# An outer product moved from VectorE into one more matmul of each of the first 32 items, with a new order of steps

## The chip, the core and the metric

The kernel runs on one core of a Trainium2 chip. The metric is device time in microseconds (us): the median of three executions, 1103.94 us, with a lowest of 1103.72 and a highest of 1105.09. The engines are called PE (TensorE matmuls), PEld (TensorE weight loads), DVE (VectorE), ACT (ScalarE), POOL (GpSimd) and SP (SyncE, which here only issues transfers).

## What is computed

The reference is a real part of a two-dimensional Fourier transform, followed by two feed-forward layers:

```
X   = fft(fft(x, axis=1), axis=2).real            # x: 2 x 3008 x 256
x1  = X.reshape(6016, 256)
h   = x1 @ w_in                                   # 256 x 2048
y   = (h * clip(h + 3, 0, 6) / 6) @ w_out         # 2048 x 256
xn  = y / sqrt(mean(y*y) + 1e-6) * rms_g
out = (silu(xn @ w_gate) * (xn @ w_val)) @ w_out2 # 256 x 1536, 1536 x 256
```

The transform along the 256 columns is folded into `w_in` (function `wmm`, L302): the 256 columns become 128 cosine-like ones and 128 sine-like ones, and one column is left over, number 128. Its contribution to the even half E of a hidden unit f is a rank-one term: (row 128 of the transformed weight at f) times (column 128 of the folded input at each token). That term is what the change is about.

## The kernel before, in words

**Precision.** Every product is made of three matmuls of split numbers (`PASSES`, L35): high part by high part, high by low, low by high. A high part is a copy rounded to the matmul type (ACT writes it), a low part is the difference (`sub`, L271, on POOL, or on DVE where a step in the list carries an apostrophe, L748).

**Stages.** First the input is folded and split (`fold`, L350, `sums`, L329), the transform's matrices are converted (`conv_mat`, L234), and small matmuls make the sequence transform (`pmm`, `xmm`, L443 to L447), evacuated by `evac` (L449) and `evac_x` (L464). Meanwhile the four 512-column chunks of `w_in` and of `w_out` are decoded from 64-bit floats on ACT and DVE (`decode`, L254) and those of `w_in` are transformed by `wmm`. Then 96 items of the first layer run (`item1`, L526): six blocks of 502 tokens by 16 groups of 128 hidden units. The order of the items (L523) is block 0 with groups 0 to 7, block 1 with all 16, block 0 with groups 8 to 15, then blocks 2 to 5. So items 0 to 31 are blocks 0 and 1. Then 144 items of the second layer follow (`item2`, L682), with `rms` (L631) between.

**One item of the first layer.** Three matmuls into a PSUM bank E and three into a bank O (L536), then on DVE T = x128 * w128 + E (L540, `scalar_tensor_tensor`, the rank-one term), E = T + O and O = T - O (L542, L543); ACT makes two Relu passes into R (L548), DVE two clip-and-multiply passes (L551), ACT the rounded copy HI (L554), POOL two subtractions into LO (L559), and 12 matmuls go from HI and LO into four accumulating banks (L570). There are two E/O pairs, two T, two R, two HI and two LO buffers, used in turn.

**Column 128.** `fold_x128`, `split_x128` and `xmm` make the transformed column in both batches at once: partitions 0 to 63 hold the first batch, 64 to 127 the second. `evac_x` writes it into `xb[0]` (tile PQX0) and issues three transfers on SP for each parity of frequencies (L476 to L478): two copy the second batch's half to both halves of `xb[1]` (tile X1), and the third overwrites the lower half of `xb[0]`, once the first two have read it. The weights of column 128 are row 0 of the bank `o` in `wmm`: ACT copies it to a T buffer (L313), SP writes it to a DRAM row (L315) and reads it back as the per-partition scalars `wx` (L322).

**The order of the work.** Every task is a Python generator, and the list `STEPS` (L78 to L166) says by hand which task takes its next step. All engines' queues get their instructions in that order. A planner wrote the list. The number alone is a step of a first-layer item, `+n` one of the second layer.

Of the kernel before, what the change touches and what calls it, by code (L numbers as in the profile page):

```python
# [76 lines left out]
}  # L77
STEPS = """  # L78
    one dm x01 x01 raw00 xq x00 x00 lwi0 raw01 raw02 x02 x02 raw11 raw10 fold1 fold1 fold1 fold1 fold1 mat00 mat00 fx
    fold1 mat00 sx0 fold0 fold1 fold0 sx0 fold1' sx0 fold0 X00 fold1 fold0 fold1 fold0 dwi0 fold1' fold0 dwi0 fold0 mat01  # L80
    fold0' mat01 dwi0 PQ100 mat01 mat02 fold0 dwi0 mat02 X01 fold0 fold2 lwi1 mat02 fold0' dwi0 PQ101 fold2 fold2 X02
    dwi0' mat11 mat11 PQ000 fold2 lwo0 evx0 fold2 wt0 mat11 mat10 evx0 wt0 mat10 fold2 evx0 mat10 PQ001 fold2 wt0 fold2'
    wt0 wt0 fold2 PQ102 wt0 wt0 fold2 wt0 PQ002 ev10 fold2' dwo0 ev10 raw12 PQ010 dwo0 ev00 wt0 ev00 PQ011 dwo0 pq00 PQ110
    mat12 dwo0 PQ111 mat12 pq00' dwo0 PQ012 mat12 dwo0' ev01 PQ112 ev01 dwi1 lwo1 0 ev11 dwi1 ev11 dwi1 1 0 sx1 dwi1 sx1
    sx1 0 dwi1 X10 1 0 dwi1 1 X11 lwi2 0 1 X12 lwi3 lwo3 wt1 0 1 pq01 0 2 evx1 1 0 evx1 wt1 dwo1 2 1 2 0 wt1 1 wt1 wt1
    dwo1 2 evx1 pq01 dwi3 2 1 dwi3 2 wt1 wt1 2 lwo2 3 g wt1 wt1 2 3 4 dwi3 2 3 dwi3 3 4 3 4 5 3 dwo1 3 4 5 4 3 5 6 4 dwo1
    4 5 3 6 dwo1 5 4 6 7 5 dwo1 6 7 7 5 4 dwi2 6 5 dwi2 7 8 dwi2 6 5 7 6 dwi2 6 9 8 7 8 7 6 9 8 7 9 8 9 7 8 9 dwi2 8 10 9
    8 7 11 10 9 10 9 8 11 10 dwi2 11 10 11 9 dwo2 11 10 dwo2 10 wt2 11 dwo2 12 10 g wt2 12 11 12 10 wt2 dwi3 11 wt2 wt2
    dwi3' 12 wt2 11 wt2 wt2 12 wt2 12 dwo2 wt3 dwo3 12 13 12 dwo2 wt3 13 13 12 wt3 lm00 wt3 dwo2' wt3 13 wt3 wt3 13 wt3
    x10 wt3 14 13 dwo3 13 15 14 14 13 15 14 13 15 14 15 dwo3 14 16 15 14 16 17 15 14 16 15 14 17 16 15 17 16 17 15 16 17  # L90
    16 dwo3 18 16 17 19 dwo3 18 18 17 16 19 17 18 19 dwo3 18 19 17 18 19 18 lf0 20 19 18 21 20 lf0 19 18 21 20 19 21 20 19
    lf0 21 20 x11 lf0 22 20 lf0 20 21 22 20 23 21 22 21 20 pq02 23 21 23 22 pq02 23 22 21 23 22 22 lf1 24 23 22 25 24 lf1
    23 22 25 24 23 25 24 23 25 24 25 24 26 23 lf1 24 27 26 x12 25 26 24 27 25 24 26 27 25 26 27 lf1 28 26 27 25 26 28 28
    26 29 lf1 27 lf2 28 27 26 29 28 27 29 30 28 lf2 29 28 27 30 29 28 30 31 29 30 29 28 31 31 29 30 31 29 30 31 30 lf2 32
    30 31 33 32 32 31 30 33 32 31 33 32 33 31 32 33 32 lf2 34 33 32 31 35 ls00 33 34 33 32 35 lf2 34 lm01 35 33 34 ls00 35
    34 35 34 36 34 35 gr00 36 34 36 35 36 34 35 ls10 36 gr00 lm02 ls10' gr00 37 36 36 38 37 37 36 35 38 37 38 37 38 36 37
    38 37 39 38 37 40 39 38 39 37 38 40 39 40 39 40 38 39 40 39 41 40 39 42 41 40 41 39 40 42 41 42 41 42 40 41 42 41 43
    42 41 44 43 42 43 41 42 44 43 44 43 44 42 43 44 43 45 44 43 gr10 45 44 45 44 45 43 lm10 gr10 45 ls01 gr10 lm11 46 pq10
    45 pq10' 47 45 46 44 47 45 46 ls01 47 46 45 47 46 47 46 48 46 47 gr01 48 47 48 46 47 48 46 lm12 gr01 48 ls11 gr01 49
    48 48 47 49 49 48 ls11' 49 50 lw00 47 49 50 gr11 49 50 49 50 49 48 50 cw00 gr11 cw00 gr11 51 50 cw00 cw00 pq11 50 52  # L100
    51 lw10 cw00 lw01 51 50 49 52 51 cw00 52 51 52 50 51 52 51 53 52 51 54 53 52 53 51 52 54 53 54 53 54 52 53 54 rms2 53
    55 54 rms2 53 56 55 55 pq11 53 56 55 56 54 cw01 55 54 cw01 57 55 56 55 54 57 56 55 57 58 56 cw01 57 cw01 56 55 58 lw11
    cw01 57 56 cw01' 59 57 58 cw10 57 56 59 58 cw10 57 59 58 57 59 cw10 58 59 58 60 cw10 59 58 61 lw20 cw10 60 60 cw10 58
    61 60 59 cw10 61 cw11 59 60 59 61 cw11 60 cw11 61 60 62 cw11 61 60 lw21 cw11 63 62 62 61 60 63 cw11 62 63 61 cw20 cw11
    62 61 63 cw20 62 cw20 63 62 64 cw20 63 62 cw20 65 64 64 63 62 65 cw20 64 65 63 cw21 cw20 64 63 65 cw21 64 cw21 65 64
    66 63 cw21 64 67 66 65 66 64 cw21 65 67 66 67 65 rms0 66 cw21 65 67 66 cw21 67 66 rms0 68 67 66 69 68 68 67 66 69 67
    68 69 68 69 67 68 69 68 70 69 68 71 70 69 70 68 69 71 70 71 70 71 69 70 71 rms0 70 rms0 72 71 70 73 72 72 71 70 73 71
    72 73 72 73 71 72 73 72 rms0 73 74 72 rms0 75 rms0 73 74 rms0 72 74 73 75 74 rms0 75 73 rms0 75 74 rms0 75 74 76 pq12
    rms0 74 77 76 75 76 74 77 75 74 76 77 75 76 pq12 77 78 76 77 75 rms1 76 78 78 76 79 rms1 77 rms0 78 77 76 79 rms0 79
    77 78 79 77 rms0 78 79 78 rms0 80 79 78 rms0 81 79 80 78 81 79 80 81 80 79 rms0 81 80 lw30 rms0 81 80 82 rms0 79 80 83  # L110
    82 82 cw30 80 81 83 80 82 cw30 81 83 81 82 cw30 81 83 cw30 82 lw40 83 82 84 83 82 85 84 83 84 82 83 85 84 85 84 85 83
    84 85 84 86 85 84 87 86 85 86 84 cw30 85 87 86 cw30' 87 85 86 87 86 87 86 88 87 86 rms1 89 88 88 tw1 86 87 89 88 87 89
# [736 lines left out]
```

## Time and profile before

| what | value |
|---|---|
| median of 3 executions | 1103.94 us (1103.72 to 1105.09) |
| the profiled execution | 1106.04 us |
| its span, first to last instruction | 1104.1 us |
| its mean granted TensorE clock | 0.992 of full speed |
| PE busy in the span | 1056.1 us, 4572 matmuls |
| DVE, ACT, POOL busy | 774.9, 537.5, 501.0 us |

Read the profile in this order: busy time by engine over the whole span, then busy time by stretch, then, for the stretch in which items 0 to 31 run, the idle time ahead of each group of matmuls and what ended it, then the chain of waits. The profiled execution is 1.94 us outside its span and 2.10 us above the median.

### The profile page before, as it was taken

How to read it: one execution, taken by the hardware profiler on the slowest of the kernel's cores; microseconds unless marked ns; L12 is line 12 of the kernel's file. 1: busy time of each engine (PE TensorE's matmuls, PEld its weight loads, DVE VectorE, ACT ScalarE, POOL GpSimd, SP SyncE). 2: the span in 40 equal slices, each digit the busy share in tenths (PEclk: the TensorE clock that was granted, in tenths of full speed). 3: DMA queues.
4: the chain of work that ended last, by engine and by line, in shares of the span. 5: the costliest groups of instructions: out<-in, count | busy, mean ns of one | idle time of the engine just before them, and what ended most of it. 6: DMA issues, size and time to landing. Idle time of an engine off the chain costs nothing.

```text
span 1104.1 us, 12691 instructions
## 1 busy us (share of the span) xinstructions
PE 1056.1 (96%) x4572; PEld 865.2 (78%) x4572; DVE 774.9 (70%) x1173; ACT 537.5 (49%) x814; POOL 501.0 (45%) x384
## 2 busy tenths in 40 slices
PE   3789898999999999999999999999999999999998
PEld 3668777888887877777878888888888888888886
DVE  7799999987889989887687574454554456364532
ACT  5556555555656666654445343333333344343332
POOL 0057477767676766654534333332323333332332
PEclk9899999999999999999999999999999999999999
DMA  8450401042502100111310000000000000000000
GB/s 294 136 173 1 80 12 65 1 83 47 129 7 96 39 0 20 39 39 44 109 58 20 19 1 20 2 17 19 1 19 1 19 8 12 19 1 20 1 19 20
DMA packets 19175, 47.21 MB, mean 43 GB/s; under 512 B 3942, under 2 KB 7014, under 8 KB 18478
## 3 DMA queue, kind: packets, MB, share of 16 engines
q1 hardware_dynamic: 16088, 36.92, 10.2%
q0 software_dynamic: 3024, 9.48, 3.8%
q8 instruction: 36, 0.59, 0.2%
q14 instruction: 27, 0.22, 0.1%
HBM read 33.53 MB, written 8.27 MB: 38 GB/s over the span
## 4 chain that ended last, share of the span: by engine, by line
PE 67%; DVE 19%; POOL 5%; issue 3%; ACT 3%; DMA 2%; SPq 0%; DVEq 0%; ACTq 0%; POOLq 0%
PE acc L715 16%; PE E L693 16%; PE O L693 16%; PE acc L570 12%; POOL LO L272 4%; PE E L536 3%; PE O L536 3%; DVE R L551 3%; DVE T L540 2%; DVE O L543 2%; DVE E L542 2%; ACT HI L554 1%; PE E L439 1%; PE O L439 1%; DMA J<-in_x 1%
## 5 line engine op out<-in xcount | busy, mean ns | idle before, releaser
L272 POOL TENSOR_TENSOR LO<-R,HI 128x502 fp32r<-128x502 f32 x192 | 260.9, 1387 | 143.9 <-ACT HI L554 143.9
L570 PE MATMUL acc<-HI,B 128*128 128x502 f32 x768 | 248.4, 392 | 0.0
L699 DVE TENSOR_TENSOR R<-T,E 128x502 f32<-128x502 f32 x144 | 97.2, 675 | 201.1 <-ACT T L696 187.7
L272 POOL TENSOR_TENSOR HI<-R,HI 128x502 fp32r<-128x502 f32 x87 | 116.6, 1340 | 231.7 <-ACT HI L705 231.5
L570 PEld LDWEIGHTS acc<-HI,B 128*128 128x128 f32 x768 | 145.4, 189 | 30.6 <-POOL B L272 0.3
L570 PE MATMUL acc<-LO,B 128*128 128x502 f32 x384 | 151.2, 394 | 2.1 <-POOL LO L272 2.0
L693 PE MATMUL E<-J,B 128*128 128x502 f32 x576 | 147.9, 392 | 1.0 <-DVE R L699 1.0
L693 PE MATMUL O<-J,A 128*128 128x502 f32 x576 | 147.5, 391 | 1.1 <-DVE R L701 1.1
L272 POOL TENSOR_TENSOR LO<-R,LO 128x502 fp32r<-128x502 f32 x57 | 76.5, 1342 | 155.7 <-ACT LO L705 155.5
L554 ACT CAST HI<-R 128x1004 fp32r<-128x1004 f32 x96 | 99.0, 1033 | 66.2 <-PE acc L570 33.1
L696 ACT ACTIVATE T<-E 128x502 f32<-128x502 f32 x144 | 84.5, 588 | 94.4 <-PE E L693 94.2
L693 PEld LDWEIGHTS E<-J,B 128*128 128x128 f32 x576 | 108.6, 189 | 25.2 <-DVE R L699 2.6
L693 PEld LDWEIGHTS O<-J,A 128*128 128x128 f32 x576 | 108.9, 189 | 24.3 <-DVE R L701 1.5
L548 ACT ACTIVATE R<-E,c_three 128x502 f32<-128x502 f32 x96 | 65.4, 681 | 98.8 <-DVE E L542 65.4
L705 ACT CAST HI<-R 128x502 fp32r<-128x502 f32 x87 | 53.4, 613 | 112.3 <-DVE R L701 91.3
L701 DVE TENSOR_TENSOR R<-R,O 128x502 f32<-128x502 f32 x144 | 97.4, 676 | 11.7
L536 PE MATMUL E<-J,A 128*128 128x502 f32 x288 | 84.8, 403 | 14.6 <-DVE R L551 10.1
L715 PE MATMUL acc<-HI,B 128*128 128x502 f32 x354 | 89.7, 390 | 0.0
L570 PEld LDWEIGHTS acc<-LO,B 128*128 128x128 f32 x384 | 72.9, 190 | 19.9 <-POOL LO L272 4.9
L536 PE MATMUL O<-J,A 128*128 128x502 f32 x288 | 83.4, 399 | 0.8 <-DVE A L320 0.8
L536 PEld LDWEIGHTS E<-J,A 128*128 128x128 f32 x288 | 53.4, 192 | 33.3 <-DVE R L551 16.7
L715 PEld LDWEIGHTS acc<-HI,B 128*128 128x128 f32 x354 | 66.9, 189 | 14.0
(234 smaller groups left out, 1605.1 us busy)
## 6 DMA issues: line engine op xcount, KB each, us to landing
out_dram<-H SPq DMA_DIRECT2D x24, 251.0 KB
A<-in_w_in SPq DMA_DIRECT2D x4, 1024.0 KB
...
```

Of the source, the lines that this page charges most:

```text
L272: low[0].tensor_tensor(o, a, b, op=ALU.subtract)
L536: T.matmul(bk[:, :BL], a[:, lw, eo, fs], j[:, eo, lx], start=(n == 0), stop=(n == 2))
L548: S.activation(x, bk[:, :BL], AF.Relu, bias=c3)
L551: V.scalar_tensor_tensor(x, x, 6.0, bk[:, :BL], op0=ALU.min, op1=ALU.mult)
L554: S.copy(hi, r)
L570: T.matmul(acc[k][:, :BL], w[:, lw, f % 4, d * P:(d + 1) * P], (hi, lo)[lx][:, hf * BL:(hf + 1) * BL], start=(first and n == 0), stop=(las ...
L693: T.matmul(bk[:, :BL], w[:, lw, d, fs], j[:, d, lx], start=(m == 0), stop=(m == 5))
L696: S.activation(s, E[:, :BL], AF.Sigmoid)
L699: V.tensor_tensor(u, s, E[:, :BL], op=ALU.mult)
L701: V.tensor_tensor(u, u, O[:, :BL], op=ALU.mult)
L705: S.copy(hl[0], u)
L715: T.matmul(acc[d][:, :BL], w[:, lw, f % 4, d * P:(d + 1) * P], hl[lx], start=(f == 0 and m == 0), stop=(f == NF2 - 1 and m == 2))
```

## The change

Part one, in `wmm`: a tile `wk` is cleared on 64 partitions (`zero_wk`, two ACT passes in all), and gets row 128 of the weights as three rows: the rounded value in partitions 0 and 32 (two ACT copies of one row), the low part in partition 1 (one small transfer issued by POOL). The bank `o` is now converted ahead of `e`.

Part two, in `evac_x`: a tile `xk` gets the first batch's column 128: ACT writes its rounded copy to 64 partitions, DVE overwrites partitions 32 to 63 with the low part. The second batch's copies are made later, by two transfers of a new task `late_x` into the slot of `xk` once items 0 to 31 are through with it, and by three transfers of 502 columns in the second `evac_x`.

Part three, in `item1`: in blocks 0 and 1 a seventh matmul, of 64 partitions, adds the rank-one term to E, and T is now a copy of E made by ACT. Blocks 2 to 5 are as before.

Part four: the list of steps is planned anew (2568 steps for 2554). Of the steps that it moves: the load `x10` goes from item 13 to ahead of item 0; `lwo3` from item 1 to ahead of item 0 and `lwi2` from item 1 to item 2; `mat01` goes ahead of `mat00`; the decoding `dwi1` and the evacuation `ev11` are finished, or nearly, ahead of item 0; the second-layer tail keeps its order in long runs.

```diff
     # wmm
-        for k, p in enumerate((e, o)):
+        for k, p in ((1, o), (0, e)):
             S.copy(a[:, 0, k], p[:, :512])
             yield
             V.tensor_tensor(a[:, 1, k], p[:, :512], f32(a[:, 0, k]), op=ALU.subtract)
             yield
+            if k == 1:
+                G.dma_start(wk[ch // 2][1:2, ch % 2], a[0:1, 1, 1])
+                yield
+                S.copy(wk[ch // 2][0:1, ch % 2], o[0:1, :512])
+                S.copy(wk[ch // 2][32:33, ch % 2], o[0:1, :512])
+                yield
...
+    def zero_wk(k):
+        wk[k] = sl(("H1", "H0")[k], [P, 2, 512], F32R)
+        S.activation(wk[k][0:64].rearrange("p a n -> p (a n)"), f32(dm[0:64]), AF.Copy, scale=0.0)
...
     # evac_x
-        cs = slice(oa, ob + n)
-        SY.dma_start(d1[0:64, cs], d0[64:128, cs])
-        SY.dma_start(d1[64:128, cs], d0[64:128, cs])
-        SY.dma_start(d0[64:128, cs], d0[0:64, cs])
+        if par == 1:
+            t = late["x2"] = sl("X1b", [P, BL])
+            SY.dma_start(t[0:64], d0[64:128, 2 * BL:])
+            SY.dma_start(t[64:128], d0[64:128, 2 * BL:])
+            SY.dma_start(d0[64:128, 2 * BL:], d0[0:64, 2 * BL:])
+            yield
+        if "k" not in xk:
+            xk["k"] = sl("X1", [P, 2 * BL], F32R)
+        cs = slice(oa, ob + n if par == 0 else 2 * BL)
+        S.copy(xk["k"][0:64, cs], d0[0:64, cs])
+        yield
+        V.tensor_tensor(xk["k"][32:64, cs], d0[32:64, cs], f32(xk["k"][32:64, cs]), op=ALU.subtract)
         done.add(("ex", par))
+    def late_x():
+        t = late["x1"] = sl("X1", [P, 2 * BL])
+        SY.dma_start(t[0:64], xb0[64:128, 0:2 * BL])
+        SY.dma_start(t[64:128], xb0[64:128, 0:2 * BL])
...
     # item1
-        yield
+        if blk < 2:
+            T.matmul(E[:, :BL], wk[f // 8][0:64, f // 4 % 2, fs], xk["k"][0:64, blk * BL:(blk + 1) * BL], start=False, stop=True)
+        yield
         t = sl(rr("T", 2), [P, BL])
-        V.scalar_tensor_tensor(t, xb[b][:, q * BL:(q + 1) * BL], wx[:, f:f + 1], E[:, :BL], op0=ALU.mult, op1=ALU.add)
+        if blk < 2:
+            S.copy(t, E[:, :BL])
+        else:
+            V.scalar_tensor_tensor(t, xcol(blk), wx[:, f:f + 1], E[:, :BL], op0=ALU.mult, op1=ALU.add)
```

## Rows read from the trace of the kernel before

**Rows 1.** The page: busy time by engine over the span, instructions.

```profile
PE 1056.1 (96%) x4572; PEld 865.2 (78%) x4572; DVE 774.9 (70%) x1173; ACT 537.5 (49%) x814; POOL 501.0 (45%) x384
```

**Rows 2.** Busy time by stretch: five of the six that cover the span.

```profile
core 0: us, PE busy (x) PEld busy (x) DVE busy (x) ACT busy (x) POOL busy (x), PEclk, DMA share, GB/s
0.00:49.00 49.00, 25.78 (x102) 22.79 (x102) 36.61 (x72) 28.60 (x40) 0.90 (x5) 0.93 0.67 221
49.00:204.00 155.00, 141.40 (x585) 112.13 (x586) 146.19 (x217) 90.94 (x127) 100.65 (x68) 0.97 0.23 66
204.00:300.00 96.00, 95.60 (x437) 80.60 (x436) 79.02 (x129) 54.14 (x79) 64.27 (x61) 1.00 0.34 71
300.00:450.00 150.00, 145.51 (x626) 116.61 (x625) 139.32 (x215) 95.95 (x135) 102.01 (x75) 1.00 0.09 32
...
530.00:1104.00 574.00, 569.47 (x2490) 469.95 (x2488) 311.20 (x453) 224.06 (x371) 189.28 (x142) 1.00 0.05 18
```

**Rows 3.** DVE's group of line 540, from 49 to 204 us.

```profile
L540 DVE SCALAR_TENSOR_TENSOR T<-PQX,c_wx,E 128x502 f32<-128x502 f32 x32 | 23.4, 730 | 3.1 <-PE E L536 3.1
```

**Rows 4.** The chain that ended last: 24 matmuls of 502 columns, back to back.

```profile
141.61 5.49 PE acc L570 x24
```

**Rows 5.** PE's groups with idle time ahead of them, from 49 to 204 us.

```profile
L536 PE MATMUL E<-J,A 128*128 128x502 f32 x96 | 29.5, 417 | 11.4 <-DVE R L551 7.0 <-DVE A L320 3.0 <-DVE PQX L461 1.4
L536 PE MATMUL O<-J,A 128*128 128x502 f32 x96 | 29.3, 416 | 0.8 <-DVE A L320 0.8
L439 PE MATMUL acc<-A,J 126*128 126x376 f32 x9 | 2.1, 356 | 1.2 <-ACT J L423 1.1
L309 PE MATMUL E<-B,LO 128*128 128x512 f32 x6 | 1.7, 413 | 0.5 <-DVE R L551 0.5
```

**Rows 6.** Busy time and granted clock of two stretches inside 49 to 204 us.

```profile
70.00:90.00 20.00, 16.59 (x57) 13.06 (x58) 18.59 (x28) 9.69 (x14) 12.12 (x8) 0.83 0.21 59
120.00:140.00 20.00, 17.13 (x67) 12.61 (x66) 19.65 (x28) 10.40 (x15) 8.46 (x9) 0.94 0.59 109
```

**Rows 7.** ACT's groups of the nearest shapes, whole span.

```profile
L696 ACT ACTIVATE T<-E 128x502 f32<-128x502 f32 x144 | 84.5, 588 | 94.4 <-PE E L693 94.2
L260 ACT ACTIVATE W<-A 128x1024 f32<-128x1024 f32 x3 | 3.4, 1139 | 0.0
L244 ACT CAST A<-PQ 126x756 fp32r<-126x756 f16 x4 | 3.1, 822 | 0.0
```

**Rows 8.** DVE's groups, whole span: its long subtraction in SBUF.

```profile
L672 DVE TENSOR_TENSOR J<-LO,J 128x1004 fp32r<-128x1004 f32 x12 | 14.4, 1198 | 0.6 <-ACT J L670 0.5
```

**Rows 9.** Timeline of POOL: the transfer that it issues at the start.

```profile
1.26 0.70 POOL L736 DMA_DIRECT2D LO<-in_dmat  x1 [0.81 <-POOLq L841]
```

**Rows 10.** Timeline of ACT: the copy of row 128 in the first chunk.

```profile
31.94 0.57 ACT L313 COPY T<-acc 1x512 f32<-1x512 f32 x1
```

**Rows 11.** The chain that ended last, 25 to 50 us: start, us, what.

```profile
30.61 0.54 SPq L476
...
31.20 3.90 DMA X<-PQX
...
35.11 0.46 SPq L478
...
35.67 1.97 DMA row<-T
...
37.74 0.48 ACT T L456
```

**Rows 12.** Who waited for whom on PE, from 210 to 500 us.

```profile
PE E L536 <- DVE R L551: 3.1, 6, 0.9
PE acc L570 <- POOL LO L272: 2.0, 5, 0.8
```

**Rows 13.** ACT's group of the HI casts, from 49 to 204 us.

```profile
L554 ACT CAST HI<-R 128x1004 fp32r<-128x1004 f32 x30 | 30.9, 1033 | 31.4 <-DVE R L551 18.0 <-PE acc L570 13.4
```

More of the change, by code (lines that the diff above doesn't have):

```diff
@@ L64 @@
     "lwi3": ("load_win", 3), "lwo0": ("load_wout", 0), "lwo1": ("load_wout", 1), "lwo2": ("load_wout", 2),
[1 row of a table removed]
-    "mat10": ("conv_mat", 1, 0), "mat11": ("conv_mat", 1, 1), "mat12": ("conv_mat", 1, 2), "one": ("consts",),
[10 rows of a table removed]
[2 rows of a table added]
+    "one": ("consts",), "pq00": ("split_pq", 0, 0), "pq01": ("split_pq", 0, 1), "pq02": ("split_pq", 0, 2),
[10 rows of a table added]
 }
 STEPS = """
-    one dm x01 x01 raw00 xq x00 x00 lwi0 raw01 raw02 x02 x02 raw11 raw10 fold1 fold1 fold1 fold1 fold1 mat00 mat00 fx
-    fold1 mat00 sx0 fold0 fold1 fold0 sx0 fold1' sx0 fold0 X00 fold1 fold0 fold1 fold0 dwi0 fold1' fold0 dwi0 fold0 mat01
@@ L81 @@
[L81 to L90, printed above, removed]
@@ L156 @@
[L156 to L160 removed]
[5 rows of a table removed]
+    one dm xq x01 x01 raw01 g raw00 x00 x00 lwi0 fx raw02 sx0 x02 sx0 x02 raw11 sx0 fold1 raw10 fold1 fold1 fold1 fold1
@@ new lines @@
+    mat01 mat01 g fold1 mat01 fold1 mat00 fold1' mat00 fold0 fold1 mat00 X00 fold0 fold1 fold0 fold1' X01 fold0 fold0 dwi0
+    fold0 fold0 dwi0 mat02 fold0' mat02 fold0 PQ100 mat02 dwi0 fold0 X02 fold2 PQ101 dwi0 evx0 lwo0 PQ000 fold2 lwi1 dwi0
+    fold2 PQ001 mat11 evx0 mat11 dwi0' evx0 fold2 wt0 zw0 evx0 mat10 fold2 wt0 mat10 dwo0 fold0' fold2 mat10 dwo0 fold2
+    wt0 fold2' mat11 wt0 fold2 PQ002 wt0 x10 dwo0 fold2 PQ102 ev00 fold2 wt0 ev00 ev10 wt0 wt0 raw12 dwo0 wt0 wt0 ev10
+    dwo0 wt0 PQ010 pq00 dwo0' PQ110 pq00' dwi1 PQ011 mat12 dwi1 PQ111 mat12 mat12 dwi1 PQ012 PQ112 dwi1 ev01 zw1 ev01 lwo1
@@ new lines @@
+    ev11 lwo3 dwi1 ev11 0 sx1 dwi1' sx1 1 0 sx1 0 X10 1 0 1 X11 0 1 X12 lwi3 0 1 wt1 lwo2 0 1 2 0 pq01 wt1 2 1 evx1 2 dwo1
+    1 evx1 wt1 2 wt1 dwo1 0 evx1 wt1 2 dwi3 wt1 lwi2 wt1 wt1 3 dwi3 wt1 2 wt1 dwi3 2 1 3 evx1 wt1 3 2 evx1 4 3 pq01 dwi3 2
+    4 3 4 3 dwo1 5 3 4 4 5 3 5 6 4 dwo1 4 5 3 6 5 dwo1 4 6 7 5 dwo1' 6 5 4 7 6 5 7 8 6 7 6 5 8 7 6 8 9 7 8 7 6 9 8 7 dwi2
+    9 10 8 dwi2 9 8 7 dwi2 10 8 9 7 dwi2 11 10 9 8 11 9 dwi2 11 9 10 dwi2 9 11 10 11 10 10 wt2 11 10 dwo2 12 11 dwo2 wt2
+    12 11 10 12 wt2 dwi3 wt2 dwo2 wt2 dwi3 12 wt2 wt2 11 wt2 12 wt2 wt2 12 wt2 dwo2 wt3 dwo3 12 13 12 dwo2 wt3 13 13 12
@@ L427, in fft_mlp_mlp_kernel @@
     pqx0 = sl("PQX0", [P, 3, NP])
-    xb = [pqx0[:, 2], sl("X1", [P, NP])]
+    xb0 = pqx0[:, 2]
+    xk = {}
+    wk = {}
+    def zero_wk(k):
+        wk[k] = sl(("H1", "H0")[k], [P, 2, 512], F32R)
+        S.activation(wk[k][0:64].rearrange("p a n -> p (a n)"), f32(dm[0:64]), AF.Copy, scale=0.0)
     pq = {0: pqx0[:, 0:2]}
@@ L524, in fft_mlp_mlp_kernel, with xcol @@
     items1 += [(n, f) for n in range(2, NB * NQ) for f in range(NF1)]
+    def xcol(blk):
+        if blk == 2:
+            return xb0[:, 2 * BL:]
+        return late["x2"] if blk == 5 else late["x1"][:, (blk - 3) * BL:(blk - 2) * BL]
     def item1(i):
@@ L535, in item1 @@
             for n, (lw, lx) in enumerate(PASSES):
-                T.matmul(bk[:, :BL], a[:, lw, eo, fs], j[:, eo, lx], start=(n == 0), stop=(n == 2))
+                T.matmul(bk[:, :BL], a[:, lw, eo, fs], j[:, eo, lx], start=(n == 0), stop=(n == 2 and (eo == 1 or blk > 1)))
+        assert all(("ex", par) in done for par in PARS[q])
+        if blk < 2:
+            T.matmul(E[:, :BL], wk[f // 8][0:64, f // 4 % 2, fs], xk["k"][0:64, blk * BL:(blk + 1) * BL], start=False, stop=True)
         yield
-        assert all(("ex", par) in done for par in PARS[q])
         t = sl(rr("T", 2), [P, BL])
-        V.scalar_tensor_tensor(t, xb[b][:, q * BL:(q + 1) * BL], wx[:, f:f + 1], E[:, :BL], op0=ALU.mult, op1=ALU.add)
+        if blk < 2:
+            S.copy(t, E[:, :BL])
+        else:
+            V.scalar_tensor_tensor(t, xcol(blk), wx[:, f:f + 1], E[:, :BL], op0=ALU.mult, op1=ALU.add)
         yield
```

143 lines of the change are left out of this document (72 added, 71 removed), and 34 rows, old and new, of tables (STEPS, TASKS).

## The prediction

> **What bounds the kernel now.** I read the page first: PE is busy 1056.1 of 1104.1 us, so the whole is a matter of matmuls, but busy is modelled and the share is an average over stages [rows 1]. The view by stretch says where PE is not the limit [rows 2]. From 530 us on PE is busy 569.5 of 574 us: nothing that the change leaves as it is can gain there. From 204 to 300 it is 95.6 of 96, with DVE at 79.0 (82%). From 49 to 204 the order is reversed: DVE is busy 146.2 of 155 us (94%) and PE 141.4, and only 585 matmuls are recorded. That stretch is the one of the change: it holds all 32 instances of the L540 form that reads the column from PQX for blocks 0 and 1, 730 ns each, 23.4 us in all [rows 3].
>
> How much PE really lacks there is counted, not read off its busy time. The chain shows 24 matmuls in 5.49 us, 0.229 us apart [rows 4]; 585 of these are 133.8 us, so 155 - 133.8 = 21.2 us pass without streaming. The groups of PE's idle time name 13.9 of them [rows 5]: 7.0 + 0.5 wait for DVE's L551 (the last DVE pass of an item, which frees a bank), 3.0 + 0.8 for L320 (the weights of a new chunk, also late on DVE), 1.4 for PQX and 1.2 for the column's operand. In two stretches the granted clock fell below full speed, to means of 0.83 and 0.94 over 20 us, a mixture of the 1.2 and the 2.4 GHz level; in both PE had gaps [rows 6]. At most 20 x 0.17 + 20 x 0.06 = 4.6 us went there. The other 2.7 us have no name in these rows.
>
> **The items: what is removed and added.** DVE loses 32 x 0.73 = 23.4 us [rows 3]. PE gains 32 matmuls of 502 columns. I price them at 0.229 each, 7.3 us, since the number of columns is that of the others; that they use 64 partitions is the rival below. ACT gains 32 copies of 502 columns from PSUM; the nearest row has 588 ns, so 18.8 us [rows 7]. ACT is busy 90.9 of 155 us in that stretch [rows 2], so this becomes 109.7 plus the small copies below, and hides, if the order of its queue allows. DVE's remaining 122.8 us and a low-part subtraction of 250 columns for the second half of `xk` (under the 1.2 us of the 1004-column one [rows 8]) fit a stretch of 149 us with 83%, the load at which PE streams unhindered from 204 to 300; at 93% (300 to 450) PE is busy 145.5 of 150 [rows 2]. So DVE stops being the pace and PE becomes it.
>
> What comes back, item by item: the waits for L551 go, 7.5 us. Those for L320 hang on DVE's order as well as on decoding, I take half of 3.8, that is 1.9. The waits for PQX and for the column's operand stay. Of the 4.6 us of clock I take half, 2.3, and of the unnamed 2.7 half, 1.3. That is 13.0, less 7.3 of new matmuls: **5.7 us gained**. Ends: all 21.2 come back, a gain of 13.9; or none, a loss of 7.3. I take the value near the middle because the 82% stretch shows PE with no loss and the decode chain is still there.
>
> A new chunk's weights now also need a transfer from POOL for partition 1. POOL issued one in 0.70 us [rows 9]; four are 2.8 us in POOL's 100.7 of 155 [rows 2], so POOL covers it. It waits for DVE's subtraction of `o`, and behind it in POOL's queue stand the LO subtractions of running items, whose matmuls PE would then wait for; that is why I let half of the L320 waits stay. Two more copies of one row cost ACT 2 x 0.57 per chunk [rows 10], 4.6 us over four chunks, in its idle time. The order of `o` and `e` is free.
>
> **The start, 0 to 49 us.** Removed are the three SP transfers of the first `evac_x`. The chain shows what they did: the third could not be issued until the first two had landed, at 35.1, and the write of the weights' row stood behind it in SP's queue until 35.67 [rows 11], although ACT had finished the row at 31.94 + 0.57 = 32.51 [rows 10]. An evacuation's T copy then waited for that write until 37.74. So 3.2 us of the path go. Added ahead of item 0 are two clearings of 1024 columns (1.14 each), a 754-column copy (0.82) [rows 7], two row copies (1.14) [rows 10] and a subtraction of 754 columns (under 1.2, [rows 8]): 4.2 us of ACT, busy 28.6 of 49, and 1.2 of DVE, busy 36.6 of 49 [rows 2]. Ends: 3.2 gained, or, with all additions on the path, 2.2 lost. I take half of the first, **1.6 gained**, because both engines have more idle time than is added.
>
> **What is moved.** `mat01` ahead of `mat00` puts three casts of 0.82 us [rows 7] in front of those that the first matmul needs; up to 2.5 us late there, but the next ones then have their operands, so I price it at nothing with 2.5 lost as its end. `dwi1` and `ev11` ahead of item 0 put DVE work of 4 to 5 us (L262 to L267 of one chunk) into a stretch where DVE has 12.4 us idle [rows 2]; it comes out of the stretch behind it. The load `x10` passes on SP's queue from item 13 to ahead of item 0, and `lwo3` moves too: they wait there for their slots, and `raw12`, `lwo1` and the rows of `wt1` stand behind them. `lwi2` comes later, still ahead of `dwi2`. The 754-column triple on SP becomes one of 502 columns in the second `evac_x`, issued behind the row of `wt1`. `late_x` issues two transfers on SP at item 31, which wait for item 31's seventh matmul; nothing of SP's is due before item 48. I price all this at nothing; with its cover gone it would cost about one wait of the size of the first `evac_x`'s, 3.2 us [rows 11]. Behind 204 us the same instructions run in nearly the same order; PE's waits from 210 to 500 us are 3.1 and 2.0 us [rows 12], so that re-planning can give at most 5.1 us and I take nothing, with as much lost at the other end.
>
> **Sum.** 5.7 + 1.6 = 7.3 us off the profiled execution, 1106.04 - 7.3 = 1098.7. That execution lies 2.1 us above the median of the runs shown, so for the median 1103.94 - 7.3 = **1096.6 us**.
>
> **Rival: the 64-partition matmul disturbs the stream (slower).** Each of the 32 matmuls stands between matmuls of 128 partitions, so PE changes shape 64 times. The trace has matmuls of 126 partitions among those of 128, never of 64. If PE must empty at each change, the price is a matmul's own length less its pitch: 0.417 - 0.229 = 0.188 us [rows 5, 4], 64 x 0.188 = 12.0 us, and 1103.94 - 7.3 + 12.0 = 1108.6 us. It turns the gain from 7.3 / 64 = 0.114 us per change on. For it: no row shows such a change for free. Against it: the weights are still 128 columns wide and the stream 502. Chance 0.2. The Trainium skill, page "TensorEngine Tiling (Array Packing)", section Key Properties, speaks for it: a change of the tiling mode, as against a change of tile, drains the TensorE. By that rule it would be this rival, if 64 partitions do set another mode; no run here shows it yet.
>
> **Rival: the wait moves to ACT (no change).** T is now made when all seven matmuls are through, 4 x 0.229 = 0.9 us later than the third, and by a queue in which the HI casts stood idle 31.4 us, 13.4 of them for PE's own accumulation [rows 13]. A copy behind such a cast holds back DVE's L542 and thus the bank. If that keeps the 7.5 us of bank waits, the time is 1103.94 - 7.3 + 7.5 = 1104.1 us. Against it: ACT's idle time. Chance 0.13.
>
> **Rival: all of the lack comes back.** 13.9 + 3.2 = 17.1 gained, 1086.8 us. Against it speaks the decoding that each new chunk still needs. Chance 0.12.
>
> **How the numbers follow.** The forecast has 0.55, with 1091 to 1101 of its own. About 0.2%, 2.2 us, is what a measurement of this kernel can tell from no change. Faster by more: 0.55, the 0.12 of the last rival and 0.03 of the second, 0.70. Within: 0.07 of the second and 0.05 of the first (a half-sized price), 0.12. Slower: 0.15 of the first and 0.03 of the second, 0.18. The range runs from 1088, just above the largest gain, to 1107, which takes in the smaller part of the first rival and all of the second.
>
> **What would show it.** Right: in the stretch of items 0 to 31 DVE falls to about 83% busy, PE's waits for L551 vanish, the clock stays at 1.00, item 31 ends about 7 us sooner, the first `wt` row is written without waiting. The start of a 64-partition matmul and of its successor 0.229 us behind their predecessors would settle the first rival; 0.4 would prove it. Wrong: PE idle ahead of L536 and ended by ACT, a later first item, or new waits after 204 us as large as the gain.

## The result, and the profile after

The changed kernel takes 1113.99 us (median of 4 runs, 1111.53 to 1115.52) where the kernel before took 1104.37 on the same chip: ratio 1.0079, 95% interval 1.0060 to 1.0099. The forecast was 1096.6 with a range up to 1107. The change costs about 8.7 us where 7.3 were to be gained.

The profiled execution took 1115.52 us, span 1113.5. On its page, the busy times that answer to [rows 1]:

```profile
PE 1069.0 (96%) x4604; PEld 868.5 (78%) x4604; DVE 760.4 (68%) x1147; ACT 560.3 (50%) x858; POOL 493.3 (44%) x384
```

DVE did lose work (14.5 us net), ACT gained 22.8 and PE 12.9 with 32 more matmuls. The stretches that answer to [rows 2] (same columns; the first holds most of the 32 items, the others are shifted with the items):

```profile
49.00:204.00 155.00, 147.42 (x587) 108.25 (x586) 118.57 (x171) 105.18 (x156) 91.77 (x65) 0.98 0.19 58
...
216.00:312.00 96.00, 96.00 (x440) 81.51 (x439) 77.78 (x127) 54.36 (x80) 64.97 (x62) 1.00 0.36 77
312.00:462.00 150.00, 146.25 (x631) 117.81 (x630) 139.20 (x217) 95.94 (x136) 100.78 (x74) 1.00 0.12 39
...
542.00:1113.00 571.00, 564.68 (x2473) 466.35 (x2471) 317.83 (x456) 223.28 (x372) 180.72 (x138) 1.00 0.05 18
```

From 49 to 204 us DVE fell from 94% busy to 76% (about 83% was forecast), and PE rose from 141.4 to 147.4 us. Yet in those 155 us PE started 587 matmuls, two more than before, though each item now needs one more: the first 32 items end later. How late each item is, by the start of DVE's addition into bank E (L581, before L542), in the profiled executions:

| item | 0 | 4 | 8 | 12 | 16 | 24 | 31 | 60 | 72 | 84 | 95 |
|---|---|---|---|---|---|---|---|---|---|---|---|
| us later than before | 0.5 | 1.9 | -0.4 | 3.7 | 7.4 | 10.6 | 12.6 | 11.6 | 11.5 | 7.6 | 8.0 |

Nearly everything is lost between items 8 and 31. Three things can be read directly. First, PE's groups with idle time ahead of them, from 45 to 216 us:

```profile
L609 PE MATMUL acc<-HI,B 128*128 128x502 f32 x226 | 76.3, 402 | 1.6 <-DVE PQX L488 1.4 <-DVE B L274 0.2
...
L570 PE MATMUL E<-J,A 128*128 128x502 f32 x96 | 28.9, 410 | 5.6 <-DVE A L322 4.8 <-DVE PQX L476 0.6 <-DVE R L590 0.2
...
L573 PE MATMUL E<-X,H 64*128 64x502 f32 x32 | 16.3, 510 | 0.0
...
L311 PE MATMUL E<-YB,LO 128*128 128x512 f32 x12 | 3.2, 402 | 0.4 <-DVE A L322 0.4
L454 PE MATMUL E<-A,B 126*128 126x376 f32 x6 | 2.4, 538 | 1.4 <-DVE PQX L476 1.4
```

The waits for an item's last DVE pass, 7.5 us in [rows 5], are down to 0.2; all these waits together fell from 13.9 to 9.0 us. The new matmul lasts 510 ns where its neighbours last about 400. PE's timeline shows what is around it (start, us):

```profile
94.31 0.85 PE L570 MATMUL E<-J,A 128*128 128x502 f32 x3
95.00 0.84 PE L570 MATMUL O<-J,A 128*128 128x502 f32 x3
95.77 0.49 PE L573 MATMUL E<-X,H 64*128 64x502 f32 x1
96.19 0.50 PE L609 MATMUL acc<-HI,B 128*128 128x502 f32 x1
96.53 0.39 PE L609 MATMUL acc<-LO,B 128*128 128x502 f32 x1
...
99.03 0.85 PE L570 MATMUL E<-J,A 128*128 128x502 f32 x3
```

Between 128-partition matmuls the pitch is 0.229 us. Here the new one starts 0.316 behind the last of O's three (the median of all 32), the next starts 0.42 later, the one after that 0.34. From one item's E to the next, 94.31 to 99.03, PE takes 4.72 us for 19 matmuls without a wait, where 19 x 0.229 = 4.35: 0.37 us more, 32 times, 11.8 us. With 7.3 us for the 32 matmuls at the usual pitch, and 4.9 us of waits less, that makes 14.2 us; from item 0 to item 31 the changed kernel loses 12.1. What removing each of these gives back is another question, which the runs below answer.

Second, the wait for the weights of a chunk (L322, which was L320 in the kernel before) grew from 3.8 to 4.8 + 0.4 us. The chain that ended last shows one such place, in the second chunk (start, us, what):

```profile
68.18 0.61 DVE A L322
...
68.82 0.57 ACT H L328
...
69.40 0.57 ACT H L329
...
70.00 0.59 ACT A L320
...
70.62 0.70 DVE A L322
...
71.37 1.03 PE E L570 x3
```

Bank E, which PE needs first, is now released last: behind `o`'s conversion and the two copies of one row.

Third, DVE now waits for ACT's copy of E. Its group of the addition into E, from 45 to 216 us:

```profile
L581 DVE TENSOR_TENSOR E<-T,O 128x502 f32<-128x502 f32 x31 | 21.1, 681 | 22.0 <-ACT T L577 21.8
```

### The profile page after: what moved, and what is told of

Read it like the earlier page. It is cut to its first block, busy times and chain, and to the rows that moved or that the text cites. A ratio compares the mean times of both kernels' runs of the same rounds, so it can differ in the third digit from the quotient of the medians.

```text
span 1113.5 us, 12765 instructions
## 1 busy us (share of the span) xinstructions
PE 1069.0 (96%) x4604; PEld 868.5 (78%) x4604; DVE 760.4 (68%) x1147; ACT 560.3 (50%) x858; POOL 493.3 (44%) x384
## 4 chain that ended last, share of the span: by engine, by line
PE 81%; DVE 12%; DMA 2%; issue 2%; ACT 2%; POOL 0%; SPq 0%; DVEq 0%; ACTq 0%
PE acc L609 19%; PE E L732 16%; PE O L732 16%; PE acc L754 16%; PE E L570 5%; PE O L570 5%; DMA A<-in_w_in 2%; DVE R L590 2%; DVE E L581 1%; PE E L573 1%; DVE O L582 1%; PE E L454 1%; PE O L454 1%; DVE T L579 1%; DVE c_p L269 1%
## 5 line engine op out<-in xcount | busy, mean ns | idle before, releaser
L581 DVE TENSOR_TENSOR E<-T,O 128x502 f32<-128x502 f32 x96 | 65.5, 683 | 27.1 <-ACT T L577 21.8
```

Of the source, the lines that this page charges most:

```text
L581: V.tensor_tensor(E[:, :BL], t, O[:, :BL], op=ALU.add)
```

## The experiments

All ratios are against runs of the kernel before, taken together with those of the run. "New" is the changed kernel's list of steps; "old" is the order of the kernel before, with the new steps put beside their neighbours.

| run | list | added matmul on | `wmm` converts first | else | ratio (95%) |
|---|---|---|---|---|---|
| changed kernel | new | 64 | o | | 1.0079 (1.0060 to 1.0099) |
| e1_full | new | 128 | o | | 1.0059 (1.0036 to 1.0081) |
| e2_twice | new | 64, twice | o | | 1.0179 (1.0154 to 1.0204) |
| e3_oldplan64 | old | 64 | o | | 1.0127 (1.0107 to 1.0147) |
| e4_oldplan128 | old | 128 | o | | 1.0074 (1.0048 to 1.0099) |
| e5_order | new | 128 | e | | 1.0032 (1.0013 to 1.0052) |
| e6_mid | new | 128 | e | matmul behind E's | 1.0024 (1.0012 to 1.0037) |
| e7_none | new | none | o | term left out | 1.0036 (1.0022 to 1.0050) |
| e8_prime | new | 128 | e | one step on DVE | 1.0029 (1.0013 to 1.0046) |
| e9_order64 | new | 64 | e | | 1.0039 (1.0026 to 1.0052) |
| e10_none_order | new | none | e | term left out | 1.0014 (1.0000 to 1.0029) |
| e11_tail | old, new behind item 31 | none | e | term on DVE | 1.0012 (0.9998 to 1.0026) |
| e12_96 | new | 96 | e | | 1.0030 (1.0014 to 1.0046) |
| e13_pure | old | none | e | term left out, no new tasks | 0.9964 (0.9945 to 0.9982) |
| e14_oldplan_order | old | 128 | e | | 0.9999 (0.9987 to 1.0010) |
| e15_pure_mm | old | 128 | e | no new tasks | 0.9975 (0.9962 to 0.9989) |
| e16_oldplan_mid | old | 128 | e | matmul behind E's | 0.9993 (0.9981 to 1.0005) |
| e17_rows_dma | old | 128 | e | and rows by DMA | 0.9981 (0.9971 to 0.9991) |
| e18_splice | new, old behind item 19 | 128 | e | | 1.0005 (0.9994 to 1.0016) |

0.1% is 1.1 us. Differences under about 0.25% between two runs of this table are not resolved one by one.

**The shape (e1, e2).** In e1 the slices `0:64` of the matmul, of the zeroing and of the copy of x become `0:P`; e2 issues the 64-partition matmul twice, so its term counts double.

```diff
-            T.matmul(E[:, :BL], wk[f // 8][0:64, f // 4 % 2, fs], xk["k"][0:64, blk * BL:(blk + 1) * BL], start=False, stop=True)
+            T.matmul(E[:, :BL], wk[f // 8][0:P, f // 4 % 2, fs], xk["k"][0:P, blk * BL:(blk + 1) * BL], start=False, stop=True)
```

> The changed kernel with the extra matmul on all 128 partitions: rows of zeros are added to its weights, the copy of column 128 is taken over 128 partitions, and the order of steps is the changed one. Theory A (the shape of 64 partitions costs: in the changed kernel's trace each extra matmul starts 0.316 us behind its predecessor, its successors start 0.42 and 0.33 us later, 0.375 us above three pitches of 0.229): the gaps fall to 0.229, and 32 x 0.375 = 12 us come back, about 1102 us. Theory B (the new order of steps costs, the matmul is innocent): within 2 us of the changed kernel's 1114.

> The changed kernel with the 64-partition matmul issued twice in a row, so that the rank-one term of blocks 0 and 1 is counted twice. Theory A (what costs is the change of shape between neighbours): the second of the pair costs a plain pitch, 32 x 0.229 = 7.3 us, about 1121 us, and the pair's inner gap is 0.23. Rival A2 (every matmul of 64 partitions costs 0.60 whatever stands beside it): 32 x 0.60 = 19 us, about 1133 us. Theory B says as A.

1112.29 and 1126.01 us. In e1 the gaps are regular: 0.2265 us ahead of the new matmul and 0.2285 behind (medians), so the 11.8 us are gone from PE's records. But by the ratios the time fell by 0.20% only, 2.2 us, which by itself is within the noise; theory A is refuted. Waits that the slow matmuls had covered came out; PE's, from 45 to 216 us:

```profile
PE E L570 <- DVE A L322: 5.0, 2, 2.8
PE E L311 <- DVE A L322: 2.9, 1, 2.9
PE E L570 <- DVE R L590: 1.9, 5, 0.5
PE acc L609 <- DVE PQX L488: 1.7, 1, 1.7
PE E L570 <- DVE PQX L476: 1.4, 1, 1.4
```

That is 12.9 us of waits where the changed kernel has 9.0, 3.9 of the 9.6 us that do not show in the time; the rest is not explained by these rows. In e2 the two 64-partition matmuls start 0.335 us apart, but the pair delays the stream of matmuls by 0.38 us in all (medians of four gaps, 1.30 us less 4 x 0.229), no more than the one does: in PE's records the second costs a plain pitch, as theory A says, and what costs is the change of shape. The time lies between the two forecasts; the granted clock from 49 to 204 us is 0.94, where the changed kernel has 0.98.

**The list of steps (e3, e4).** e3 is the changed kernel with the old list, e4 the same with 128 partitions.

```diff
-    one dm xq x01 x01 raw01 g raw00 x00 x00 lwi0 fx raw02 sx0 x02 sx0 x02 raw11 sx0 fold1 raw10 fold1 fold1 fold1 fold1
...
+    one dm x01 x01 raw00 xq x00 x00 lwi0 raw01 raw02 x02 x02 raw11 raw10 fold1 fold1 fold1 fold1 fold1 mat00 mat00 fx
...
```

> The changed tasks in the order of steps of the kernel before, with the new steps put right behind their neighbours; 64 partitions. Theory A: the price of the shape stays, 12 us; what comes back is the later first item (52.35 us against 49.20), at most 3 to 5 us, so 1109 to 1114 us. Theory B: the loss goes with the new order, so about 1097 to 1104 us.

> As the run before it, with the matmul on 128 partitions. Theory A: 12 us below the run before it, 1097 to 1102 us, the first version under the kernel before. Theory B: the same time as the run before it.

1119.82 and 1113.17 us; both forecasts of e3 and both of e4 missed. As it stands, the new list is better than the old one by 0.5% at 64 partitions; that the new order alone costs the time is refuted. In the old list the shape costs 0.5%. Neither explains why even e1 and e4 lose 6 to 8 us.

**The order in `wmm` (e5, e9).** Both products are converted in the old order, E first; the DMA and the row copies come behind both, and the copies read the converted block. So this is one edit of three parts, and no run tells the order of the conversions from the place of the two row copies. (For the waits on L322, the expectation gives the kernel before 0.8 us; [rows 5] has 3.0 + 0.8.)

```diff
-        for k, p in ((1, o), (0, e)):
+        for k, p in enumerate((e, o)):
...
-                S.copy(wk[ch // 2][0:1, ch % 2], o[0:1, :512])
-                S.copy(wk[ch // 2][32:33, ch % 2], o[0:1, :512])
+        S.copy(wk[ch // 2][0:1, ch % 2], f32(a[0:1, 0, 1]))
+        S.copy(wk[ch // 2][32:33, ch % 2], f32(a[0:1, 0, 1]))
```

> Edit: e1_full (the changed kernel with the added matmul on all 128 partitions, nothing else) with the four products of a block of wmm converted in the old order, E before O; the row DMA and the two row copies come behind both, and the copies read the converted block instead of the bank. As many steps as before. Theory C (in e1_full the gain is eaten by wmm: bank E is released last, behind o and the row copies, and PE waits 5.0 us on L322 in its items and 2.9 us on L322 in the next block's matmuls, where the kernel before had 0.8 and none): most of these 7 us come back, 4 to 6 us below e1_full, about 1107. Theory D (the order is no matter, the waits follow from how the steps are planned): within 1.5 us of e1_full, about 1112.

> Edit: the changed kernel (added matmul on 64 partitions) with wmm's order put back as in e5_order; the fourth corner of the square of shape and order. Theory additive (shape and order cost on stretches of their own): the changed kernel less the 3.1 us that the order gave at 128 partitions, about 1111, and 1.7 us above e5_order. Theory cover (PE, slowed by the shape, is late anyway, so what wmm releases later is hidden, and the other way round): within 1 us of the changed kernel, 1113 to 1114, so the shape costs 4 to 5 us once the order is right.

1109.22 and 1110.26 us. At 64 partitions the order is worth 0.40%, and the intervals part. At 128 it is 0.27%, less than forecast and by itself within the noise. PE's waits in e5, 45 to 216 us:

```profile
PE E L568 <- DVE R L588: 5.9, 8, 1.9
...
PE O L568 <- DVE A L322: 0.4, 1, 0.4
PE E L311 <- DVE A L322: 0.3, 1, 0.3
...
PE E L568 <- DVE A L322: 0.2, 1, 0.2
```

The waits for L322 fell from 7.9 to 0.9, as theory C has it, but 4 us of them reappear as waits for the last pass of an item. With the order right, 64 partitions cost 0.07% more than 128, which is not told apart from nothing: most of the 11.8 us in PE's records fall into time in which PE would wait anyway. The ten runs of e5 fall into two groups, five of 1106.2 to 1107.7 us with a granted clock of 0.995 to 0.997, and five of 1110.8 to 1111.9 with 0.991 or 0.992; its profile is one of the first group.

**What the matmul costs (e7, e10), and which shapes disturb (e12).** e7 is the changed kernel without the added matmul, e10 is e5 without it; e12 is e5 with `0:96` for `0:P`.

```diff
-        if blk < 2:
-            T.matmul(E[:, :BL], wk[f // 8][0:64, f // 4 % 2, fs], xk["k"][0:64, blk * BL:(blk + 1) * BL], start=False, stop=True)
```

> Edit: the changed kernel without the added matmul; the term of column 128 of the first two blocks is left out of the result, the zeroing, the row copies and ScalarE's copy of E stay. It shows what taking the term off VectorE is worth when PE pays nothing for it. Theory P (PE's rate is what the first two blocks are bound by): the changed kernel less 32 x 0.604 = 19.3 us (0.375 for the change of shape, 0.229 for the matmul), about 1094.7. Theory Q (the stage is bound by the banks and by the waits of wmm, the matmuls only fill waiting time): e1_full less at most 3 us, 1109 to 1112.

> Edit: e5_order without the added matmul; the term of column 128 of the first two blocks is left out of the result. It is the most that relieving VectorE could give with the right order. Theory P (32 more matmuls on a PE that is full in most of the stage cost their time): e5_order less 5 to 7.3 us (32 x 0.229), about 1103. Theory Q (VectorE's other work of the stage, the decoding and the sums, and the waits of wmm bound it, the matmuls stand in waiting time): within 2 us of e5_order, 1107 to 1109.

> Edit: e5_order with the added matmul, the zeroing and the copy of x on 96 partitions instead of 128 (rows 64 to 95 are zeros against data, as rows 64 to 127 were). Theory H1 (what costs is a tile of at most half the rows): gaps of 0.229 us around it as at 128, time within 1 us of e5_order. Theory H2 (any matmul on fewer rows than its neighbours breaks the row of matmuls): start 0.316 after its predecessor and next one 0.42 later as at 64, time as e9_order64.

1109.01, 1107.71 and 1109.07 us. Theory P falls twice: with nothing at all to pay on PE, neither is faster than the kernel before (e10's interval just reaches it). The bound is not PE's rate. On 96 partitions the gaps are 0.2265 and 0.231 us, as on 128, so theory H1 holds.

**Smaller suspects (e6, e8, e11).** e6 issues the matmul right behind E's three; e8 gives the subtraction of `dwi3` back to DVE, by the mark on its step; e11 is the kernel before with the new list behind item 31 (no other edit).

```diff
+            if blk < 2 and eo == 0:
+                T.matmul(E[:, :BL], wk[f // 8][0:P, f // 4 % 2, fs], xk["k"][0:P, blk * BL:(blk + 1) * BL], start=False, stop=True)
...
-    12 11 10 12 wt2 dwi3 wt2 dwo2 wt2 dwi3 12 wt2 wt2 11 wt2 12 wt2 wt2 12 wt2 dwo2 wt3 dwo3 12 13 12 dwo2 wt3 13 13 12
+    12 11 10 12 wt2 dwi3 wt2 dwo2 wt2 dwi3' 12 wt2 wt2 11 wt2 12 wt2 wt2 12 wt2 dwo2 wt3 dwo3 12 13 12 dwo2 wt3 13 13 12
```

> Edit: e5_order with the added matmul issued right behind E's three matmuls, ahead of O's three, so that bank E is whole 3 matmuls (0.69 us) earlier and ScalarE's copy of it runs beside O's matmuls. Theory F (the longer chain of an item, PE E to ACT copy to DVE to ACT to DVE, is what PE ends up waiting for, seen as waits on the product of DVE, 5.4 us in e1_full): 2 to 4 us below e5_order. Theory C (only the order of wmm counts): within 1 us of e5_order.

> Edit: e5_order with one letter of the list of steps: the subtraction of dwi3 goes back to VectorE, where the kernel before had it; the changed list gives it to GpSimd (2.4 us), and a shift of VectorE beside it took 3.0 us instead of 1.2. Theory G (the slow pair delays the release of bank E and the block wt3 by about 2 us): 1.5 to 2.5 us below e5_order. Rival: VectorE is given 1.2 us more at the same place, which takes it back: within 1 us of e5_order or up to 1 us slower.

> Edit: the kernel before, with its own list of steps up to the last step of item 31 and the changed kernel's list for all that comes behind it (two steps of the old list move behind that point); nothing of the term of column 128 is changed. In the profiles the changed kernel is 11.2 us late at item 36, 8.0 at item 95 and 9.4 at the end. Theory T (the new order of the later part is a gain of its own, which hides a part of what the first 32 items lose): 1.5 to 3 us below the kernel before, ratio 0.997 to 0.9985, so the first 32 items lose 2 to 3 us more than the total shows. Rival (the later part only catches up because work was pushed out of the first part): within 0.7 us of the kernel before.

1108.12, 1108.64 and 1106.48 us. None is told apart from its reference (e6 and e8 from e5, e11 from the kernel before). So the later list is no gain over the whole, but it does move time: in e11's profile item 60 comes 1.7 us later than before, item 95 1.5 earlier, and the end is 1.0 later again. Every profile with the new list there regains 3.2 to 3.6 us between items 60 and 95, none with the old list there regains more than 0.3. The 4 us that items 72 to 84 regain in the changed kernel are thus the later list's, and 1.4 of them are lost again behind item 95.

**The relief by itself (e13, e15).** One line of the kernel before: for the first two blocks ACT copies bank E, the term is left out. e15 adds a fourth 128-partition matmul with stand-in operands.

```diff
-        V.scalar_tensor_tensor(t, xb[b][:, q * BL:(q + 1) * BL], wx[:, f:f + 1], E[:, :BL], op0=ALU.mult, op1=ALU.add)
+        if blk < 2:
+            S.copy(t, E[:, :BL])
+        else:
+            V.scalar_tensor_tensor(t, xb[b][:, q * BL:(q + 1) * BL], wx[:, f:f + 1], E[:, :BL], op0=ALU.mult, op1=ALU.add)
```

> Edit: the kernel before with one line changed: in the first 32 items ScalarE copies bank E to `T` where VectorE added the term of column 128; that term is left out of the result for the first two blocks. List of steps, wmm and all else are those of the kernel before; there is no added matmul. It is the prediction's first step by itself, VectorE relieved of 32 x 0.655 = 21.0 us. Theory R (the step was right: PE's waits on VectorE come back, and other parts of the change eat it): 8 to 13 us below the kernel before, 1092 to 1097. Theory S (the copy on ScalarE only moves the wait, since the next additions of the item still stand behind it and the decoding fills VectorE's bursts anyway): within 3 us of the kernel before, 1102 to 1108.

> Edit: e13_pure with a fourth matmul of E on 128 partitions in the first 32 items (a product of the low parts of weights and data stands in for the term, so the result is off by that); no zeroing, no row copies, no new task on any other engine. Theory P (PE is the bound, the matmul costs its pitch): e13_pure plus 7.3 us (32 x 0.229). Theory S (the matmuls stand in waiting time): e13_pure plus 0 to 2.5 us, as e10_none_order to e5_order.

1100.54 and 1101.38 us: the relief is worth 0.36%, between the two theories and nearer to S, and the matmuls cost 0.11% (within the noise) where their pitch would make 0.66%. Where the freed time went stands in DVE's groups of e13, 45 to 216 us:

```profile
L545 DVE TENSOR_TENSOR E<-T,O 128x502 f32<-128x502 f32 x34 | 23.1, 679 | 17.8 <-ACT T L541 17.5
```

Of the 23.4 us of operations taken off DVE [rows 3] (21 us by the 0.65 us from the start of one to the next operation), it spends 17.5 waiting for the copy that replaced them. The timelines of ACT and of DVE show how (ACT's first; start, us):

```profile
85.25 1.07 ACT L504 CAST B<-W 128x1024 fp32r<-128x1024 f32 x1
86.33 1.03 ACT L557 CAST HI<-R 128x1004 fp32r<-128x1004 f32 x1
87.27 0.68 ACT L551 ACTIVATE R<-E,c_three 128x502 f32<-128x502 f32 x1
87.84 0.67 ACT L551 ACTIVATE R<-O,c_three 128x502 f32<-128x502 f32 x1
88.40 0.57 ACT L541 COPY T<-E 128x502 f32<-128x502 f32 x1
```

```profile
86.44 0.67 DVE L546 TENSOR_TENSOR O<-T,O 128x502 f32<-128x502 f32 x1
89.01 0.69 DVE L545 TENSOR_TENSOR E<-T,O 128x502 f32<-128x502 f32 x1 [1.90 <-ACT T L541]
```

The copy stands in ACT's queue behind a cast of decoded weights, a HI cast and the two passes of the item before, and DVE stands still for 1.90 us; PE's three matmuls into that bank E had ended at 86.97. PE's waits from 45 to 216 us, first of e13:

```profile
PE E L536 <- DVE R L554: 4.5, 5, 1.9
PE E L536 <- DVE A L320: 4.0, 2, 3.0
PE acc L573 <- POOL B L272: 1.4, 1, 1.4
PE E L536 <- DVE PQX L461: 1.3, 2, 0.7
```

and those of e15:

```profile
PE E L536 <- DVE A L320: 2.8, 1, 2.8
PE E L536 <- DVE PQX L461: 1.1, 2, 0.6
PE acc L575 <- POOL B L272: 1.0, 1, 1.0
PE E L536 <- DVE R L556: 0.9, 3, 0.4
```

With the rest of each view, e13 waits 12.7 us and e15 7.0. So the relief alone hardly shortens the waits (13.9 in [rows 5]); the new matmuls then stand in 5.7 us of them. What did change in e13's profile is the clock (columns as above; compare [rows 2] and [rows 6]):

```profile
49.00:204.00 155.00, 142.10 (x611) 113.11 (x610) 132.16 (x190) 109.12 (x163) 103.35 (x69) 1.00 0.22 66
70.00:90.00 20.00, 14.04 (x58) 10.78 (x59) 18.07 (x26) 13.32 (x20) 12.37 (x8) 1.00 0.23 63
120.00:140.00 20.00, 17.32 (x73) 13.06 (x72) 17.27 (x25) 13.42 (x20) 9.59 (x10) 1.00 0.48 110
```

By the prediction's own count, 611 matmuls of 0.229 us leave 15.1 of 155 us without streaming, where 585 left 21.2. The waits explain 1.2 of these 6.1 us, and the clock, which had cost up to 4.6, most of the others. That is one execution of each kernel; over all runs beside each other the mean granted clock is 0.9957 in e13 and 0.9941 in the kernel before, 1.8 us of 1104, so how the 4.0 us divide between clock and waits is open.

**Old list and right order (e14), and where the new list loses (e18).** e14 is e4 with e5's edit of `wmm`; e18 is e5 with the old list behind the last step of item 19.

> Edit: e4_oldplan128 (changed kernel, added matmul on 128 partitions, the old list with the new steps put beside their neighbours) with wmm's E block converted before O, as in e5_order. If the order's cost is one of wmm and not of the list: 3 us below e4_oldplan128, about 1110. If the new list is the one that loses in the first 32 items once the order is right: below e5_order, 1104 to 1107.

> Edit: e5_order with the old list (that of e14_oldplan_order) for all that comes behind the last step of item 19; ahead of it stands the new list (one step of item 20 moves behind the point). In the profile e5_order loses 6.9 us against the kernel before between items 20 and 26 (from 4.6 ahead to 2.3 behind), e14_oldplan_order 0.5. Theory L (the new list loses in the decoding behind item 19): 3.5 to 5 us below e5_order, about 1105, level with e14_oldplan_order. Rival (the old list would lose there as well, once it comes behind the new list's first part): within 1.5 us of e5_order.

1104.51 us, ratio 0.9999: in the old list the order of `wmm` is worth 0.75%, and with E first the new list is 0.33% worse than the old. e18 comes to 1105.81, 0.27% below e5, a little under what theory L wants; in its profile items 20 to 26 lose 3.1 us against the kernel before, where e5 loses 6.9 and e14 0.5. The stretch 160 to 200 us (columns as above), first of e5, then of e14:

```profile
160.00:200.00 40.00, 38.83 (x168) 30.68 (x167) 37.74 (x54) 25.70 (x38) 26.10 (x18) 1.00 0.15 52
```

```profile
160.00:200.00 40.00, 39.77 (x175) 32.45 (x174) 34.84 (x57) 27.55 (x42) 28.47 (x20) 1.00 0.15 52
```

The new list has other DVE work in there, 2.9 us more in these 40 us, and PE starts 7 matmuls fewer. From 45 to 216 us PE waits for an item's last DVE pass for 5.9 us in e5 (L588, above); the same line in e14:

```profile
PE E L571 <- DVE R L591: 0.5, 2, 0.3
```

Which of the list's steps does it was not tried.

**A version that beats both (e16, e17).** e16 is e14 with the matmul behind E's three; e17 also brings rows 0 and 32 of `wk` by POOL's DMA queue instead of two ACT copies.

```diff
-        S.copy(wk[ch // 2][0:1, ch % 2], f32(a[0:1, 0, 1]))
-        S.copy(wk[ch // 2][32:33, ch % 2], f32(a[0:1, 0, 1]))
+        G.dma_start(wk[ch // 2][0:1, ch % 2], a[0:1, 0, 1])
+        G.dma_start(wk[ch // 2][32:33, ch % 2], a[0:1, 0, 1])
```

> Edit: e14_oldplan_order with the added matmul right behind E's three, ahead of O's. A complete kernel that may beat both. Theory F (the longer chain from E over ScalarE to VectorE still makes waits): 1 to 2 us below e14_oldplan_order, 1102.5 to 1103.5, ratio about 0.9985. Theory S (PE's waits that are left there, 3.3 us on wmm's subtraction, 1.1 on PQX and 1.6 on GpSimd's low parts, have nothing to do with that chain): within 0.7 us of it, 1104 to 1105.

> Edit: e16_oldplan_mid with rows 0 and 32 of wk brought by two more DMAs from GpSimd's queue, like row 1, instead of two copies on ScalarE. ScalarE has 8 x 0.57 = 4.6 us less in the first 32 items, GpSimd 8 x 0.53 = 4.2 us more. If ScalarE's small copies are a part of the 3 us by which e14_oldplan_order stands above e15_pure_mm: 1 to 2 us below e16_oldplan_mid. Rival: GpSimd's low parts come later and PE waits for them: 0 to 2 us above it.

1104.14 and 1103.19 us, beside 1104.97 for the kernel before. e17, a complete kernel, is faster than both: ratio 0.9981, interval 0.9971 to 0.9991, some 2 us. The step from e16 to e17 (0.12%) has the forecast sign and is not resolved by itself, nor is that from e14 to e16 (0.06%).

## Why the prediction was wrong

The sign is wrong because the relief of DVE gave far less than it was priced at, while the edits beside it, priced at nothing, cost more than that. The runs make a path from the kernel before to the changed one, each step one edit or group of edits. By the ratios, in us of 1104.4:

| step | us | priced in the prediction at |
|---|---|---|
| the term off DVE, copied by ACT (e13) | -4.0 | -13.0 |
| 32 matmuls at the usual shape (e13 to e15) | +1.2 | +7.3 |
| zeroing, row copies, POOL's DMAs, `xk` (e15 to e14) | +2.7 | -1.6, the start included |
| the new list (e14 to e5) | +3.6 | 0, with ends of 2.5, 3.2 and 5.1 for its parts |
| `o` and the row copies ahead of `e` (e5 to e1) | +3.0 | 0 |
| 64 partitions for 128 (e1 to the changed kernel) | +2.2 | 0, 12.0 in a rival |
| sum | +8.7 | -7.3 |

Each step carries 2 to 3 us of uncertainty, so the second and the last two are not clear of noise on this path; and the split depends on the path, since the costs hide one another (the order is worth 0.75% in the old list, the shape 0.5% there, both clear of noise). What is firm is the first step and that list, order and shape together make the difference between e14 (0.9999) and the changed kernel (1.0079).

**"The waits for L551 go, 7.5 us."** This is the step that failed first: the relief was priced at 13.0 us and gave 4.0. The mechanism was half right: DVE did fall to 76%, and the clock of the two stretches of [rows 6], 0.83 and 0.94 there, is 1.00 in both in e13 (in the changed kernel 0.91 and 0.92), so that term, priced at 2.3, came back in these profiles. But a wait for the last DVE pass is a wait for the whole chain ahead of it, and that chain went from E, DVE to E, ACT, DVE. In e13 4.8 of the 7.5 us of those waits remain, the waits for L320 are 4.8 us where half of 3.8 was to go, and DVE idles 17.5 us on the copy. In the changed kernel itself the waits for the last pass are down to 0.2, as forecast, but only while the slow matmuls and the wait for L322 hold PE up: they are 1.9 in e1 and 5.9 in e5. It was the second rival, the wait that moves to ACT, with a chance of 0.13, that described this; "against it: ACT's idle time" was the wrong measure, since the copy waited for what stood ahead of it in ACT's queue (85.25 to 88.40 us above), while ACT was busy only 109.1 of 155 us.

**7.3 us for the matmuls** was too high by about 6: PE paid for most of them in time in which it waited anyway. Both terms together gave 2.8 us instead of 5.7, so they do not turn the sign.

**"The order of `o` and `e` is free"** is the step that failed most plainly. Bank E is what PE's next item asks for, and the chain at 68 us shows it released as the last of five instructions, two of which are the row copies that were to run "in its idle time". Four pairs of runs have the same sign (0.27, 0.40, 0.22 and 0.75%, the third e7 to e10), the second and the last clear of noise. They move order and row copies together.

**The list priced at nothing**: 3.6 us, inside the stated ends, but neither in the start nor in SP's queue nor behind 204 us, where the prediction put those ends: it lies behind item 19, where DVE is 94% busy in e5 (160 to 200 us). Behind 204 us the new list gives 3.2 to 3.6 us between items 60 and 95 and loses 1.4 to 2.5 behind item 95.

**"Two more copies of one row … in its idle time"**, the clearings and the rest: 2.7 us together. The gain at the start, 1.6, is not to be seen: item 0 comes 0.5 us later than before in the changed kernel, and between 1.1 earlier and 0.8 later in nine of the ten experiments that begin with the new list (4.4 later in e8); in e13, whose start is the old one, it comes 1.4 later, so this is within the spread of single executions. The wait on SP's queue [rows 11] did go from the chain that ended last, but from 40.49 to 44.75 us the chain now passes subtractions, evacuations and a decoding on DVE, and item 0's first matmul starts at 52.35 us where it started at 49.20.

**The first rival** had the place and the price: 64 changes at 0.188 are 12.0 us, and the records show 11.8. The Trainium skill, page "TensorEngine Tiling (Array Packing)", section Key Properties, says that a change of the tiling mode drains the TensorE; the trace agrees for 64 partitions (0.37 us for one matmul or for two in a row), and e12 shows that 96 are no such change. What the rival had wrong is what these are worth where PE waits: 2.2 us here, 0.8 with the order right, 5.8 in the old list, of which only the last is clear of noise. No run has 64 partitions in the old list with the order right, so whether the shape alone would have made the change slower is open.

The range was too narrow because edits with small costs (order, list, small copies) were each priced at nothing, without ends or with ends of 2 to 5 us that the range up to 1107 does not add up; here they all fell on the same side and make 9.3 us together.
